# A kernel's opening: phase pieces shared by two selector halves, the first fold ahead of the transposes' copies, eight chunks' rate rows loaded first, 34 exponentials ahead of the transposes

## The chip, the cores and the metric

The kernel runs on one core of a Trainium2 chip. The core has five engines that run side by side, each through its own list of instructions in order: TensorE (PE, matrix products and transposes), VectorE (DVE), ScalarE (ACT), GpSimd (POOL) and SyncE (SP), which here only starts transfers. ACT and POOL start transfers too, and a transfer then runs on the core's DMA engines. Engines meet through semaphores, set by a scheduler that knows which tile each instruction reads and writes.

The metric is the time of one execution in microseconds of device time; less is better. Of the kernel before, three timed runs and one profiled execution are at hand.

## What is computed

The reference is one layer with its gradients. With `xn` the layer norm of `A_u` (2048 tokens, 576 channels):

```python
logdA = dt * (A_re + 1j * A_im)                  # dt = exp(log_dt), 576 x 128
K = einsum("dn,dnl,dn->dl", Cc, exp(logdA * l), dt * Bc).real   # l = 0..2047
s = irfft(rfft(xn) * rfft(K)) + xn * Dskip       # a convolution along the tokens
g = silu(silu(xn @ w1) * (xn @ w3) @ w2)         # 576 -> 4608 -> 576
out = x + s * g
```

Twelve gradients by a given `grad_out` follow, for `A_u`, the eight parameters of the state space part and the three weights. Inputs and outputs are bf16.

## The kernel before

The work has four stages, one behind the other on PE: an opening called `prologue`, the forward of both branches woven together (`ffn_hidden` with `ssm_forward`), the output product with the backward's start, and the backward. Only the opening is touched. It prepares what the forward needs:

- **Magnitudes.** The kernel `K` needs `exp(rate * l)` for 36 chunks of 16 channels. `l` is split into a coarse and a fine part, and a matrix product with a selector (`SELR`, tile `sel_dl`) spreads the rates over both. The rates are cut into three bf16 pieces (`split_rates`), written to the DRAM scratch `PCS_dram`, and read back with another layout into `LR_` (tile `lhs_r`), 48 rows by 36 chunks. `early_exps` then makes 54 blocks: two products (PE, `e_ps`), one exponential (ACT, `E_k`), one store (SP, `E_dram`). Chunks up to `TWICE` = 8 use rows 0 to 47 with a second product, the later ones also rows 64 to 111, which a fourth transfer (`lhs_r<-lhs_r`) copies from the first.
- **Phases.** `param_phases` reduces `A_im * dt / 2 pi` to turns (`thr`). For the two halves of the forward's selector (`SEL`, made by `build_selectors`) it also needs 64 times that, reduced again (`th64`). Both are cut into three pieces by `split3`, on DVE, and written to `PCS_dram` rows 0 and 1 by POOL. The forward reads them as `lhs_t` in `ssm_kernel`.
- **Layer norm.** Even token blocks are loaded straight (`xt<-in_A_u`), odd ones reversed by way of the DRAM scratch `odd_A_u`, on POOL's queue. DVE takes statistics (`ln_stats`, first the even, later the odd ones), roots them, and scales 16 tiles into `xn_bf`. `ln_turn` transposes them (PE into `t_ps`, two buffers; DVE copies `xnT<-t_ps`), ten groups `c` of them, and `ln_fold(b)` makes sums and differences of token blocks (`xt<-xn_bf`, two instructions).
- **Spectra.** `early_spectrum(n)`, n = 0 to 15, makes two groups of eight products from the folded tiles, each group copied out by DVE (from `t_ps`) or ACT (from `e_ps`); here such a group is called a half.

The order is written out by hand. `self.V`, `self.S` and `self.sy` are chains: what is called on them keeps the order of the code on DVE, ACT and SP. `lead` chains the products on PE in the same way. `early_exps` is a generator: `TURN` = 30 of its 54 steps come first, with one surplus product each, then one step behind each transposed group (10) and one behind each half of a spectrum (14, seven spectra). After that come `WT` (two groups of transposes, eight ACT instructions) and the nine spectra that are left; then PE takes up the forward with `pg<-wmB_w,xnT`.

Since PE's order is fixed, a transposed group that waits for a free `t_ps` buffer holds up all exponentials' products behind it.

Of the kernel before, what the change touches and what calls it, by code (L numbers as in the profile page):

```python
# [11 lines left out]
ALU = mybir.AluOpType  # L12
# [86 lines left out]


class K:
    LEAD, SPAN, KG, TURN, TWICE = 1, 38, (4, 6.9), 30, 8
    BACK = ((49, 0), (54, 0), (64, 2), (69, 1))

    def __init__(self, tc, aps: dict, dbg: dict | None = None):
# [208 lines left out]
    def prologue(self, matp, selp, xp, gate):  # L314
# [12 lines left out]
        with pool(name="par_tmp", bufs=1) as tmp, pool(name="par_pc", bufs=2) as pcp, pool(name="sel_tmp", bufs=1) as st, \  # L327
# [32 lines left out]
            rho = tmp.tile([P, DT, N], FP32, name="rho")  # L360
            mul(self.V, rho, self.A_re, dt_b)
            pc = self.split_rates(tmp, rho)
            for k in range(3):
                self.sy.dma_start(out=LR_[k * 16:(k + 1) * 16], in_=self.PCS_dram[2, k].rearrange("(k p) n -> p k n", p=16))
            self.sy.dma_start(out=LR_[64:112, self.TWICE:], in_=LR_[0:48, self.TWICE:])
            pw = eps.tile([P, 1024], FP32, name="e_ps")
            for k in range(16):
# [17 lines left out]
            self.ln_root([*range(LT)], small, last)  # L385
            self.ln_scale(even)
            self.ln_scale(odd)
            self.param_weights(tmp, dt_b, gq)
            self.dma_engines, self._dma_i = [self.sy], 0
            exps = self.early_exps(SELR, LR_, ep, eps)  # L390
# [5 lines left out]
            for k, tiles in enumerate((even, odd)):  # L396
                for c, _ in enumerate(self.ln_turn(tiles, tps)):
                    next(exps)
                    if 5 * k + c == 6:
                        self.ln_fold(0)  # L400
            self.pre(44)
            for n in range(7):
                if n in (2, 5):
                    self.ln_fold(1 + n // 5)
                for _ in spectrum(n, 1, 1):
                    next(exps, None)
            for _ in exps:
# [6 lines left out]
            for src, dsts in ((self.Wr, ((0, 0, 1.0 / 512), (1, 1, -1.0 / 512))), (self.Wi, ((0, 1, -1.0 / 512), (1, 0, -1.0 / 512)))):  # L414
# [3 lines left out]
                for (v, r, sc) in dsts:  # L418
                    for h in range(2):
                        self.S.mul(out=WT[:, v].rearrange("p e r h d u -> p r h e d u")[:, r, h],  # L420
                                   in_=pt[:, h * D // 2:(h + 1) * D // 2].rearrange("p (e d) -> p e d", d=2)[:, :, :, None]
                                   .to_broadcast([P, D // 4, 2, 2]), mul=sc)
            for n in range(7, 16):
                if n == 10:
                    self.ln_fold(3)
                for _ in spectrum(n, int(n < 10), int(n != 10)):
                    pass

    def param_weights(self, tmp, dt_b, q):
# [12 lines left out]
    def param_phases(self, tmp, dt_b):  # L442
        nc, DT, N = self.nc, self.cfg.DT, self.cfg.N
        V = self.V
        thp = tmp.tile([P, DT, N], FP32, name="thp", tag="t1")
        V.scalar_tensor_tensor(out=thp[:], in0=self.A_im[:], scalar=1.0 / (2 * PI), in1=dt_b, op0=ALU.mult, op1=ALU.mult)
        yield
        t = tmp.tile([P, DT, N], FP32, name="sr_t", tag="sr_r1")
        thr = tmp.tile([P, DT, N], FP32, name="thr", tag="rho")
        V.tensor_scalar(out=t[:], in0=thp[:], scalar1=MAGIC, scalar2=-MAGIC, op0=ALU.add, op1=ALU.add)  # L450
        yield
        V.tensor_tensor(out=thr[:], in0=thp[:], in1=t[:], op=ALU.subtract)
        yield
        th64 = tmp.tile([P, DT, N], FP32, name="th64", tag="t1")
        V.tensor_scalar(out=t[:], in0=thr[:], scalar1=64.0, scalar2=MAGIC, op0=ALU.mult, op1=ALU.add)
        yield
        V.tensor_scalar(out=t[:], in0=t[:], scalar1=-MAGIC, scalar2=None, op0=ALU.add)
        yield
        V.scalar_tensor_tensor(out=th64[:], in0=thr[:], scalar=64.0, in1=t[:], op0=ALU.mult, op1=ALU.subtract)
        yield  # L460
        for q, src in enumerate((thr, th64)):
            pc = self.pcp.tile([P, 3, DT, N], BF16, name="pc")
            for _ in self.split3(tmp, src, pc):
                yield
            for dst, part in self.split_rows(q, pc, slice(0, 3)):
                nc.gpsimd.dma_start(out=dst, in_=part)

    def split3(self, tmp, r, pc):
        for k in range(3):
# [107 lines left out]
    def build_selectors(self, st, selp):  # L577
        cfg = self.cfg
        AV, BV, DC = cfg.AV, cfg.BV, 16
        QW, PW = DC * BV, DC * AV  # L580
        val = self.sel_dl
        self.SEL = selp.tile([P, 2, QW // 2 + PW], BF16, name="SEL")
        o = QW + 2 * PW
        self.V.scalar_tensor_tensor(out=val[:, o:], in0=val[:, o:], scalar=self.sel_pm[:, 0:1], in1=self.sel_val[:, o:],
                                    op0=ALU.is_equal, op1=ALU.mult)
        rq = st.tile([P, 1], FP32, name="rq")
        rp = st.tile([P, 1], FP32, name="rp")
        rc = st.tile([P, 1], FP32, name="rc")
        self.V.tensor_scalar(out=rq[:], in0=self.pcol[:], scalar1=48.0, scalar2=None, op0=ALU.is_lt)
        self.V.tensor_scalar(out=rp[:], in0=self.pcol[:], scalar1=64.0, scalar2=None, op0=ALU.is_ge)  # L590
        self.V.tensor_scalar(out=rc[:], in0=self.pcol[:], scalar1=112.0, scalar2=None, op0=ALU.is_lt)
        self.V.tensor_tensor(out=rp[:], in0=rp[:], in1=rc[:], op=ALU.mult)
        self.V.tensor_tensor(out=rp[:], in0=rp[:], in1=rq[:], op=ALU.add)
        rs = st.tile([P, 2], FP32, name="rs")
# [101 lines left out]
    def ssm_kernel(self, T0, TK, ps, ps1):  # L696
        nc, cfg = self.nc, self.cfg
        D, N = cfg.D, cfg.N
        AV, BV = cfg.AV, cfg.BV
        DC = 16  # L700
        NCH = D // DC
        TW = DC * (AV + BV)
        GE = 6
        assert NCH % GE == 0 and AV == 2 * cfg.LT
        with self.pool(name="kg_e", bufs=4) as ep, \
                self.pool(name="kg_l", bufs=2) as lp, \
                self.pool(name="kg_qv", bufs=4) as qvp, \
                self.pool(name="kg_sb", bufs=2) as sb, self.pool(name="kg_dft", bufs=1) as dp, \
                self.pool(name="kg_ks", bufs=2) as self.ksp:
            prev, Es, LT_ = [], [], None  # L710
            self.marks = []
            for ch in range(NCH):
                yield T0 + TK * ch
                self.at(T0 + TK * ch)
                if ch == 10:
                    self.dft_phase_rows(dp)
                if ch in (16, 20, 24, 28):
                    self.dft_kernel_tile(ps, (ch - 16) // 4)
                while len(Es) < min(ch + 3, NCH):
                    c = len(Es)  # L720
                    self.at(T0 + TK * (ch - 0.5) if ch else T0)
                    if c % GE == 0:
                        LT_ = lp.tile([P, GE, N], BF16, name="lhs_t")
                        nc.gpsimd.memset(LT_[:], 1.0)
                        for k in range(3):
                            for q, r0 in enumerate((0, 64)):
                                nc.sync.dma_start(out=LT_[r0 + k * DC:r0 + (k + 1) * DC],
                                                  in_=self.PCS_dram[q, k, c * DC:(c + GE) * DC, :].rearrange(
                                                      "(k p) n -> p k n", p=DC))
                    E = ep.tile([P, TW], BF16, name="E_l")  # L730
                    el = nc.sync.dma_start(out=E[:], in_=self.E_dram[c // 2, :, c % 2 * TW:(c % 2 + 1) * TW])
                    if c == 0:
                        self.kg_load = el
                    if c in (8, 18, 20, 22, 24):
                        self.conv_loads(el, (8, 18, 20, 22, 24).index(c))
                    Es.append((E, LT_))
                self.at(T0 + TK * ch)
                E, lhs = Es[ch]
                qv = self.kgen_chunk(ch, E, lhs[:, ch % GE, :], self.SEL, sb, qvp, ps)
                prev.append(qv)  # L740
                if ch >= 2:
                    self.kgen_sum(ch - 2, prev.pop(0), ps1, T0 + TK * ch, TK)
            for i in range(2):
                yield T0 + TK * (NCH + 0.5 * i)
                self.kgen_sum(NCH - 2 + i, prev.pop(0), ps1, T0 + TK * (NCH + 0.5 * i), TK * 0.5)
# [1514 lines left out]
```

## Time and profile before

| What | us |
|---|---|
| three timed runs: lowest, median, highest | 1645.04, 1669.88, 1679.92 |
| the profiled execution, its own time | 1652.46 |
| its span, first to last instruction | 1650.7 |
| PE busy in it | 1574.6 |
| the opening: start to the first `pg` product | 96.10 |

The rows that the argument rests on are shown where it uses them. A row of the timeline has the start in us, the duration from first to last of a merged group, the engine, the line of the kernel (L86 and L674 are helpers through which the chains issue), what is written and read, and how many instructions (x). In brackets stands the idle time of that engine just before, and what ended it. "PEclk" is the granted clock of TensorE as a share of the full one.

### The profile page before, as it was taken

To read this page: it belongs to the slowest core of one execution; us is meant where nothing else is said; L and a number is where in the kernel's file an instruction comes from. 1 tells how busy PE (TensorE), PEld (TensorE's weight loads), DVE (VectorE), ACT (ScalarE), POOL (GpSimd) and SP (SyncE) were. 2 spreads that over 40 slices of the span, in tenths; PEclk is the share of its full clock that TensorE was granted. 3 is DMA by queue.
4 is the path that set the end of the run, shared out by engine and by line. 5 is a ranking of instruction groups with operands and counts; after the bars stand their busy time and mean duration, and the time that the engine had idled before them with its cause. 6 is when DMAs were issued, how large, how long until landed. Compare 5 with 4: busy or idle time off the path is not lost. (4 is left out here: it accounts for less than half of the span.)

```text
span 1650.7 us, 34338 instructions
## 1 busy us (share of the span) xinstructions
PE 1574.6 (95%) x13327; PEld 1148.8 (70%) x13327; DVE 1390.7 (84%) x2150; ACT 836.4 (51%) x1517; POOL 474.0 (29%) x778
## 2 busy tenths in 40 slices
PE   6899999999999999999999999989999998999997
PEld 2454444444457777788888888878888876888875
DVE  9879999799966656998969999679999945788887
ACT  6789999766642116556565565545555401000101
POOL 7746766532342110111110111111111233123131
PEclk9999999999999999999999999999999999999999
DMA  7899999998999997676695756899998999999991
GB/s 229 313 334 374 378 370 384 380 271 246 325 280 220 240 208 214 173 228 192 186 270 159 217 184 179 197 226 264 246 234 247 234 235 246 233 223 238 231 239 52
DMA packets 621038, 408.57 MB, mean 248 GB/s; under 512 B 424555, under 2 KB 562235, under 8 KB 616267
## 3 DMA queue, kind: packets, MB, share of 16 engines
q1 hardware_dynamic: 565184, 274.01, 66.2%
q0 software_dynamic: 33472, 114.23, 20.7%
q10 hardware_dynamic: 22218, 18.14, 3.8%
q8 instruction: 104, 1.70, 0.4%
q14 instruction: 60, 0.48, 0.1%
HBM read 128.52 MB, written 189.06 MB: 192 GB/s over the span
## 5 line engine op out<-in xcount | busy, mean ns | idle before, releaser
L1961 PEld LDWEIGHTS <-xn_bf 128*128 128x128 bf16 x2304 | 224.3, 98 | 36.4 <-issue 10.2
L2016 PEld LDWEIGHTS <-acts 128*128 128x128 bf16 x1970 | 192.3, 98 | 48.3 <-issue 0.2
L1520 DVE TENSOR_TENSOR pr_q<-et_ps,pz 128x1024 f32<-128x1024 f32 x144 | 175.9, 1222 | 39.1 <-PE et_ps L1515 23.0
L1946 POOL DMA_DIRECT2D out_dram<-gw x72 | 47.2, 656 | 538.0 <-ACT gw L1963 318.6
L1117 PEld LDWEIGHTS <-xnT 128*128 128x128 bf16 x1152 | 107.7, 98 | 127.4 <-issue 20.1
L1523 DVE TENSOR_REDUCE S_all<-pr_q 128x32 f32<-128x1024 f32 x144 | 175.2, 1217 | 3.2
L1895 PE MATMUL ph<-w2T,goT 128*128 128x256 bf16 x1440 | 172.2, 274 | 1.6 <-ACT gh L1898 1.6
L2016 PE MATMUL px<-wT,acts 128*128 128x288 bf16 x1242 | 160.9, 287 | 0.0
L1117 PE MATMUL pg<-wmB_w,xnT 128*128 128x512 bf16 x576 | 155.9, 379 | 1.1 <-DVE g_t L1136 0.6
L1895 PEld LDWEIGHTS <-goT 128*128 128x128 bf16 x1440 | 140.0, 98 | 20.0 <-issue 3.1
L1936 PE MATMUL pgw<-go_o,h_n 128*128 128x288 bf16 x1152 | 152.3, 286 | 1.1 <-ACT gw L1942 1.0
L1117 PE MATMUL pu<-wmB_w,xnT 128*128 128x512 bf16 x576 | 149.7, 379 | 0.0
L1961 PE MATMUL pgw<-gu_n,xn_bf 128*128 128x256 bf16 x1152 | 133.5, 272 | 5.3 <-ACT gw L1942 4.8
L1936 PEld LDWEIGHTS <-h_n 128*128 128x128 bf16 x1152 | 111.9, 98 | 29.2 <-issue 2.1
L1961 PE MATMUL pgw<-gg_n,xn_bf 128*128 128x256 bf16 x1152 | 130.2, 273 | 0.4 <-ACT gw L1963 0.4
L1898 ACT CAST gh<-ph 128x512 bf16<-128x512 f32 x144 | 80.7, 589 | 89.5 <-PE ph L1895 82.2
L1132 ACT ACTIVATE s_t<-pg 128x512 bf16<-128x512 f32 x144 | 88.3, 613 | 54.5 <-PE pu L1126 42.3
L2135 ACT ACTIVATE go<-gx 128x576 bf16<-128x576 f32 x15 | 10.2, 683 | 181.6 <-DVE gx L2085 172.8
L807 POOL COPY KT<-k_s 64x128 bf16<-64x128 bf16 x144 | 85.0, 590 | 52.0 <-ACT k_s L804 47.3
L2016 PE MATMUL px<-wA,acts 128*128 128x288 bf16 x728 | 96.3, 288 | 0.0
L1137 ACT CAST u_t<-pu 128x512 bf16<-128x512 f32 x144 | 87.3, 606 | 6.2 <-PE pu L1117 6.2
L1146 POOL DMA_DIRECT2D G_dram<-g_t x72 | 51.5, 715 | 116.5 <-ACT g_t L1134 91.7
(331 smaller groups left out, 3189.2 us busy)
## 6 DMA issues: line engine op xcount, KB each, us to landing
U_dram<-u_t POOLq DMA_DIRECT2D x72, 256.0 KB, 6.0
H_dram<-h_t SPq DMA_DIRECT2D x72, 256.0 KB
G_dram<-g_t POOLq DMA_DIRECT2D x72, 256.0 KB, 5.8
Q_dram<-q_k SPq DMA_DIRECT2D x36, 512.0 KB
gg_n<-G_dram POOLq DMA_DIRECT2D x18, 1024.0 KB, 6.7
h_n<-U_dram POOLq DMA_DIRECT2D x18, 1024.0 KB, 8.8
GG_dram<-gg_n SPq DMA_DIRECT2D x36, 512.0 KB
GU_dram<-gu_n SPq DMA_DIRECT2D x36, 512.0 KB
```

What stands on the lines that cost most here:

```text
L807: nc.gpsimd.tensor_copy(out=KT[64 * hf:64 * hf + 64, :, ch // 9, h, d1:d1 + 8], in_=ks[64 * h:64 * h + 64, :, h, hf].rearrange("p d a -> p ...
L1117: ins = nc.tensor.matmul(pt[:], lhsT=xnT[:, c, ts], rhs=wm[w][:, c, :], start=(q == 0 and c == 0), stop=(q == 1 and c == nfull - 1))
L1132: nc.scalar.activation(out=s_t[:, :, q, :], in_=pgv, func=ACT.Silu)
L1137: self.gate_last = nc.scalar.copy(out=u_t[:, :, q, :], in_=puv)
L1146: self.u_stores[step] = nc.gpsimd.dma_start(out=dst[fb * ng:(fb + 1) * ng, :, i0:i0 + NT, :].rearrange("g p t f -> p g (t f)"), in_=src[:] ...
L1520: nc.vector.tensor_tensor(out=pr[:].rearrange("p r k e -> p r (k e)"), in0=T[x][:].rearrange("p z k h j a -> p (z k h j a)")[:, None].to_b ...
L1523: nc.vector.tensor_reduce(out=self.S_all[:].rearrange("p r (h c) -> p r h c", h=2)[:, :, :, d0:d0 + 2], in_=pr[:].rearrange("p r k (h j a) ...
L1895: self.pe_last = nc.tensor.matmul(ph[j][:, k, :].rearrange("p (a f) -> p a f", f=P), lhsT=lw, rhs=rh, start=(n == 0), stop=(n == nfull))
L1898: self.sc(lambda: nc.scalar.copy(out=gh[:, j], in_=ph[j][:]))
L1936: self.pe_last = nc.tensor.matmul(pgw[pi_][:, 0:pw], lhsT=hn[:, tt, fl * P:(fl + 1) * P], rhs=go_o[:, tt, po:po + pw], start=(tt == 0), st ...
L1961: self.pe_last = nc.tensor.matmul(pw_[:, 0:FG], lhsT=self.xn_bf[:, tt, c * P:(c + 1) * P], rhs=nat[:, tt, :], start=(tt == 0), stop=(tt == ...
L2016: self.pe_last = nc.tensor.matmul(px[pi_][:, 0:pw], lhsT=acts[i][:, ai, fi, :], rhs=w[:, po:po + pw], start=(n == 0), stop=(n == len(steps ...
```

## The change

```diff
-    LEAD, SPAN, KG, TURN, TWICE = 1, 38, (4, 6.9), 30, 8
+    LEAD, SPAN, KG, TURN, TWICE = 1, 38, (4, 6.9), 34, 8
...
-            for k in range(3):
-                self.sy.dma_start(out=LR_[k * 16:(k + 1) * 16], in_=self.PCS_dram[2, k].rearrange("(k p) n -> p k n", p=16))
+            for c0, c1 in ((0, self.TWICE), (self.TWICE, D // 16)):
+                for k in range(3):
+                    self.sy.dma_start(out=LR_[k * 16:(k + 1) * 16, c0:c1],
+                                      in_=self.PCS_dram[2, k, 16 * c0:16 * c1].rearrange("(k p) n -> p k n", p=16))
...
             self.ln_scale(odd)
+            self.ln_fold(0)
             self.param_weights(tmp, dt_b, gq)
...
                     next(exps)
-                    if 5 * k + c == 6:
-                        self.ln_fold(0)
             self.pre(44)
-            for n in range(7):
-                if n in (2, 5):
-                    self.ln_fold(1 + n // 5)
+            for n in range(5):
+                if n == 2:
+                    self.ln_fold(1)
                 for _ in spectrum(n, 1, 1):
                     next(exps, None)
...
-            for n in range(7, 16):
-                if n == 10:
-                    self.ln_fold(3)
-                for _ in spectrum(n, int(n < 10), int(n != 10)):
+            for n in range(5, 16):
+                if n in (6, 10):
+                    self.ln_fold(n // 4 + 1)
+                for _ in spectrum(n, int(n < 8), int(n != 10)):
                     pass
...
-        th64 = tmp.tile([P, DT, N], FP32, name="th64", tag="t1")
-        V.tensor_scalar(out=t[:], in0=thr[:], scalar1=64.0, scalar2=MAGIC, op0=ALU.mult, op1=ALU.add)
+        pc = self.pcp.tile([P, 3, DT, N], BF16, name="pc")
+        for _ in self.split3(tmp, thr, pc):
+            yield
+        for dst, part in self.split_rows(0, pc, slice(0, 3)):
+            nc.gpsimd.dma_start(out=dst, in_=part)
+        p1 = self.pcp.tile([P, 3, DT, N], BF16, name="pc")
+        t = tmp.tile([P, DT, N], FP32, name="sr_t", tag="sr_r1")
+        V.tensor_scalar(out=t[:], in0=pc[:, 0], scalar1=64.0, scalar2=MAGIC, op0=ALU.mult, op1=ALU.add)
...
-        V.scalar_tensor_tensor(out=th64[:], in0=thr[:], scalar=64.0, in1=t[:], op0=ALU.mult, op1=ALU.subtract)
+        V.scalar_tensor_tensor(out=p1[:, 0], in0=pc[:, 0], scalar=64.0, in1=t[:], op0=ALU.mult, op1=ALU.subtract)
         yield
-        for q, src in enumerate((thr, th64)):
-            pc = self.pcp.tile([P, 3, DT, N], BF16, name="pc")
-            for _ in self.split3(tmp, src, pc):
-                yield
-            for dst, part in self.split_rows(q, pc, slice(0, 3)):
-                nc.gpsimd.dma_start(out=dst, in_=part)
+        for dst, part in self.split_rows(1, p1, slice(0, 1)):
+            nc.gpsimd.dma_start(out=dst, in_=part)
...
+        self.V.tensor_scalar(out=rs[:, 0:1], in0=self.pcol[:], scalar1=80.0, scalar2=63.0, op0=ALU.is_ge, op1=ALU.mult)
+        self.V.tensor_tensor(out=rp[:], in0=rp[:], in1=rs[:, 0:1], op=ALU.add)
...
-                                                  in_=self.PCS_dram[q, k, c * DC:(c + GE) * DC, :].rearrange(
+                                                  in_=self.PCS_dram[q if k == 0 else 0, k, c * DC:(c + GE) * DC, :].rearrange(
```

The factor 64 of the second and third piece goes into the selector (two more instructions of one column in `build_selectors`), so only the first piece is reduced and stored again.

On DVE, in `param_phases`, the order changes as follows (`pc` is the tile of pieces, `sr_r` the rest that is still to be cut; `sr_t` holds whole turns).

```order
-L86 SCALAR_TENSOR_TENSOR th_343<-thr,sr_t 128x640
-L86 CAST pc<-thr 128x640
-L86 TENSOR_TENSOR sr_r_349<-thr,pc 128x640
-L86 CAST pc<-sr_r_349 128x640
-L86 TENSOR_TENSOR sr_r_352<-sr_r_349,pc 128x640
-L86 CAST pc<-sr_r_352 128x640
-L86 CAST pc<-th_343 128x640
-L86 TENSOR_TENSOR sr_r_363<-th_343,pc 128x640
-L86 CAST pc<-sr_r_363 128x640
-L86 TENSOR_TENSOR sr_r_366<-sr_r_363,pc 128x640
-L86 CAST pc<-sr_r_366 128x640
+L86 SCALAR_TENSOR_TENSOR pc<-pc,sr_t 128x640
```

The five instructions that cut `th` are gone, the cut of `thr` (removed here) now stands ahead of the reduction, and what is reduced goes straight into a piece; the odd tiles' statistics follow directly in both.

On DVE again, between the scaling and the spectra, first before, then after (`xt_152` is token block 0, `xt_153` block 1 and so on).

```order
L86 TENSOR_SCALAR xn_bf<-xt_155,rstd,negmr 128x576 x2
L86 MEMSET Wr 128x1
L86 MEMSET Wi 128x1
L86 COPY xnT<-t_ps 128x8x128 x4
L86 CAST xnT<-t_ps 128x8x128
L86 COPY xnT<-t_ps 128x8x128 x2
L86 TENSOR_TENSOR xt_152<-xn_bf 128x1152 x2
L86 COPY xnT<-t_ps 128x8x128 x2
L86 CAST xnT<-t_ps 128x8x128
L86 CAST u_e<-t_ps 128x2x288 x4
L86 TENSOR_TENSOR xt_153<-xn_bf 128x1152 x2
L86 CAST u_e<-t_ps 128x2x288 x6
```

```order
L86 TENSOR_SCALAR xn_bf<-xt_155,rstd,negmr 128x576 x2
L86 TENSOR_TENSOR xt_152<-xn_bf 128x1152 x2
L86 MEMSET Wr 128x1
L86 MEMSET Wi 128x1
L86 COPY xnT<-t_ps 128x8x128 x4
L86 CAST xnT<-t_ps 128x8x128
L86 COPY xnT<-t_ps 128x8x128 x4
L86 CAST xnT<-t_ps 128x8x128
L86 CAST u_e<-t_ps 128x2x288 x4
L86 TENSOR_TENSOR xt_153<-xn_bf 128x1152 x2
L86 CAST u_e<-t_ps 128x2x288 x8
L86 TENSOR_TENSOR xt_154<-xn_bf 128x1152 x2
```

The fold of block 0 moved from between the seventh and the eighth copy to ahead of the first, and the fold of block 2 (`xt_154`) now follows eight casts instead of six.

On SP the rates come in two groups of three loads; before there were three, and the copy into rows 64 to 111 stood right behind them. This is the order now.

```order
L86 DMA lhs_r<-PCS_dram 16x8x128 x3
L86 DMA lhs_r<-PCS_dram 16x28x128 x3
L674 DMA E_dram<-E_k 128x1024 x3
L86 DMA lhs_r<-lhs_r 48x3584
L674 DMA E_dram<-E_k 128x1024 x32
```

The copy `lhs_r<-lhs_r` is now issued behind the stores of the first three exponentials. On PE and ACT nothing in the forward or behind it changes its order.

More of the change, by code (lines that the diff above doesn't have):

```diff
@@ L588, in build_selectors @@
         rc = st.tile([P, 1], FP32, name="rc")
+        rs = st.tile([P, 2], FP32, name="rs")
         self.V.tensor_scalar(out=rq[:], in0=self.pcol[:], scalar1=48.0, scalar2=None, op0=ALU.is_lt)
@@ L591, in build_selectors @@
         self.V.tensor_scalar(out=rc[:], in0=self.pcol[:], scalar1=112.0, scalar2=None, op0=ALU.is_lt)
+        self.V.tensor_scalar(out=rs[:, 0:1], in0=self.pcol[:], scalar1=80.0, scalar2=63.0, op0=ALU.is_ge, op1=ALU.mult)
+        self.V.tensor_tensor(out=rp[:], in0=rp[:], in1=rs[:, 0:1], op=ALU.add)
         self.V.tensor_tensor(out=rp[:], in0=rp[:], in1=rc[:], op=ALU.mult)
         self.V.tensor_tensor(out=rp[:], in0=rp[:], in1=rq[:], op=ALU.add)
-        rs = st.tile([P, 2], FP32, name="rs")
         self.V.tensor_scalar(out=rs[:, 0:1], in0=self.pcol[:], scalar1=112.0, scalar2=192.0, op0=ALU.is_equal,
```

## The prediction

> **What bounds the kernel, and what bounds its opening.** I read the page first, then the busy time by stretches.
>
> ```profile
> span 1650.7 us, 34338 instructions
> PE 1574.6 (95%) x13327; PEld 1148.8 (70%) x13327; DVE 1390.7 (84%) x2150; ACT 836.4 (51%) x1517; POOL 474.0 (29%) x778
> ...
> 100.00:350.00 250.00, 247.35 (x1714) 111.11 (x1713) 230.93 (x374) 225.07 (x453) 153.94 (x243) 1.00 1.02 365
> ```
>
> A row of the stretches gives, after the limits, the length, then PE, weight loads, DVE, ACT and POOL busy, then the granted clock, the share of the DMA engines and GB/s. Behind the opening PE is busy nearly all the time (247.35 of 250 us in this stretch, 95% of the span with the opening in it), in an order that the change leaves alone. So the change is worth what it moves the first forward product on PE, and that shift passes to the end.
>
> Next I read ACT's timeline in the opening, since 54 exponentials are its longest work.
>
> ```profile
> 16.59 1.28 ACT L86 ACT_TABLE_LOAD   x1
> 19.81 1.02 ACT L86 ACTIVATE E_k<-e_ps 128x1024 bf16<-128x1024 f32 x1 [1.95 <-PE e_ps L674]
> 21.95 1.02 ACT L86 ACTIVATE E_k<-e_ps 128x1024 bf16<-128x1024 f32 x1 [1.11 <-PE e_ps L674]
> ...
> 46.61 7.71 ACT L86 ACTIVATE E_k<-e_ps 128x1024 bf16<-128x1024 f32 x8 [0.37 <-ACT E_k L86]
> 56.14 6.67 ACT L86 ACTIVATE E_k<-e_ps 128x1024 bf16<-128x1024 f32 x7 [1.81 <-issue]
> 66.64 1.02 ACT L86 ACTIVATE E_k<-e_ps 128x1024 bf16<-128x1024 f32 x1 [3.83 <-issue]
> 68.45 1.02 ACT L86 ACTIVATE E_k<-e_ps 128x1024 bf16<-128x1024 f32 x1 [0.79 <-PE e_ps L674]
> 70.26 4.95 ACT L86 ACTIVATE E_k<-e_ps 128x1024 bf16<-128x1024 f32 x5 [0.79 <-PE e_ps L674]
> 75.83 5.68 ACT L86 ACTIVATE E_k<-e_ps 128x1024 bf16<-128x1024 f32 x6 [0.62 <-PE e_ps L674]
> 82.58 1.94 ACT L86 ACTIVATE E_k<-e_ps 128x1024 bf16<-128x1024 f32 x2 [1.06 <-DMA E_dram<-E_k]
> ```
>
> One exponential takes 7.71/8 = 0.964 us in a row of them. The 54 start at 19.81 and end at 84.52. The two large holes, 1.81 and 3.83 us, are to be explained by PE and DVE.
>
> ```profile
> 9.91 6.54 PE L368 MATMUL e_ps<-pc 128*128 128x512 bf16 x16 [6.60 <-DVE pc L86]
> 18.78 1.43 PE L674 MATMUL e_ps<-sel_dl,lhs_r 128*128 128x512 bf16 x4 [2.32 <-DMA lhs_r<-PCS_dram]
> ...
> 52.54 0.59 PE L674 MATMUL e_ps<-sel_dl,lhs_r 128*128 128x512 bf16 x2
> 55.01 0.61 PE L674 MATMUL t_ps<-ident_bf,xn_bf 128*128 128x128 bf16 x8 [1.88 <-DVE xnT L86]
> 64.52 1.06 PE L674 MATMUL t_ps<-ident_bf,xn_bf 128*64 128x128 bf16 x16 [2.90 <-DVE xnT L86]
> 95.60 0.66 PE L674 MATMUL t_ps<-xt,cCS 128*128 128x144 bf16 x8
> 96.10 1.03 PE L1117 MATMUL pg<-wmB_w,xnT 128*128 128x512 bf16 x4
> ...
> 33.16 0.76 DVE L86 CAST pc<-th 128x640 bf16<-128x640 f32 x1
> 36.81 0.80 DVE L86 BATCH_NORM_STATS2 stats<-xt 128x6 f32<-128x288 bf16 x2
> 54.28 0.68 DVE L86 COPY xnT<-t_ps 128x1024 bf16<-128x1024 bf16 x1
> 60.07 3.79 DVE L86 TENSOR_TENSOR xt<-xn_bf 128x1152 bf16<-128x1152 bf16 x2
> 63.79 1.27 DVE L86 COPY xnT<-t_ps 128x1024 bf16<-128x1024 bf16 x2
> 72.52 1.42 DVE L86 TENSOR_TENSOR xt<-xn_bf 128x1152 bf16<-128x1152 bf16 x2
> 86.19 4.49 DVE L86 CAST u_e<-t_ps 128x576 bf16<-128x576 f32 x6 [2.84 <-PE t_ps L674]
> ```
>
> Both holes are PE's waits for a DVE copy. The first copy starts at 54.28, when the scaling is done, and PE's third transposed group 0.73 us later. The second wait is the fold at 60.07, 3.79 us between two copies. A third wait, 2.32 us, stands at the start, for the rates.
>
> **The parts of the change.**
>
> *Eight chunks first.* PE's surplus products end at 16.45 (9.91 + 6.54) and ACT is free at 17.87 (16.59 + 1.28). Eight of 36 chunks are 2/9 of the bytes, so I estimate the rates there by 16.5: the first exponential comes at 17.9 instead of 19.81. The second then also loses its wait of 1.11. The bounds are 0 (the load's time is all latency) and 1.95 + 1.11 = 3.1; I take 3.0. Three more loads on SP, and the copy `lhs_r<-lhs_r` behind three stores, come before the 13th exponential, the first to read it, with some 8 us to spare. By itself this part is worth nothing: what ends last next is DVE.
>
> *The phase pieces.* From 33.16 to 36.81 DVE cuts `th`; these 3.65 us go, and the two instructions of one column that are added are much less. But behind them stand the odd tiles' statistics, and POOL tells when these tiles land:
>
> ```profile
> 30.77 2.83 POOL L86 DMA_DIRECT2D xt<-odd_A_u  x4
> ...
> DMA to landing us min/median/max: 5.9/6.5/7.0
> ```
>
> The first is issued at 30.77 and lands 5.9 us later at the earliest, at 36.7; DVE's statistics began at 36.81, with no wait only because DVE came no sooner. So DVE comes 3.6 us earlier and waits 3.6 us. The gain is between 0 and 3.6, I take 0: nothing in the change makes these transfers start earlier. Exponentials that start 3 us earlier also send their stores earlier, against the same transfers. I add 0.6 us for that (0 to 1.4, the middle; 1.4 is the time of two stores' 512 KB at the 365 GB/s of the row 100 to 350).
>
> *The fold ahead of the copies.* It takes 1.42 (row 72.52) to 3.79 (row 60.07). The 3.79 stood beside POOL's products of the weights:
>
> ```profile
> 55.32 2.15 POOL L855 IOTA ph_f<- 1x256 bf16 x1
> 58.49 1.40 POOL L86 TENSOR_TENSOR Wr<-C_re_bf,B_re_bf 128x640 f32<-128x640 bf16 x1
> ```
>
> At 55 to 57 POOL still writes constants of one row, so I take 1.42. The first copy then starts at 54.28 + 0.6 + 1.42 = 56.3, and the third transposed group at 57.0. The second hole goes altogether.
>
> *34 exponentials.* Four more come ahead of the transposes, 4 x 0.964 = 3.86 us of ACT, and their four surplus products hide in PE's waits for ACT. PE's last product ahead of the wait ended at 52.54 + 0.59 = 53.13; now at 53.13 + 3.86 - 3.0 = 54.0. PE then waits from 54.0 to 57.0, which is 3.0 us.
>
> What such a wait costs beyond itself is told by the granted clock, by single microseconds:
>
> ```profile
> 54.00:55.00 1.00, 0.00 (x0) 0.00 (x0) 1.00 (x5) 0.32 (x1) 0.87 (x4) 1.00 0.98 377
> ...
> 64.00:65.00 1.00, 0.48 (x10) 0.48 (x11) 1.00 (x2) 0.00 (x0) 1.00 (x2) 0.50 1.09 358
> 70.00:71.00 1.00, 1.00 (x11) 0.88 (x10) 0.15 (x2) 0.74 (x1) 1.00 (x2) 0.77 0.66 254
> ```
>
> Behind the wait of 1.88 the clock stayed full; behind that of 2.90 it was at half by 64 and until about 70.5, and ACT's exponentials came every 1.81 us (66.64, 68.45, 70.26). A wait of 3.0 us is past the second, so I take the half clock, with the same cost: from the copy at 63.79 to the exponential at 66.64 are 2.85 us, then two steps of 1.81. The Trainium skill's page "TensorE: Matmul & The Clock Gate", section "What's actually happening", lets the clock fall after an idle window of about 3.4 us that runs free of the kernel. The trace does not bear that out as it stands, since 2.90 us were enough. By that rule the clock would stay full here, which is the first rival below.
>
> *Spectra.* Four halves move behind the exponentials. PE takes 0.50 us for one there (95.60 to 96.10), so 2.0 us. The fold of block 2 now stands among six casts that DVE did without a break (4.49 us, row 86.19): 1.42 at most, 0 if other work covers it; DVE sets the pace there, so I take 1.4.
>
> **The sum.** Exponential 37 starts at 56.3 + 2.85 = 59.15, the 39th at 62.8. Then 16 x 0.964 = 15.4 and the two small holes of before, 0.62 and 1.06: they end at 79.9, against 84.52. From their end to the first `pg` there were 11.58 us; now 11.58 + 2.0 + 1.4 = 15.0. The forward starts at 94.9 instead of 96.10, so 1.2 us are gained. Against the profiled execution's own 1652.46 that is 1651.3. That execution lies 17 us below the median of the timed runs (1669.88), and those spread over 35 us for reasons that this profile does not show. I refer the forecast to the middle of the four times, (1652.46 + 1669.88) / 2 = 1661.2, and get 1660.0.
>
> **Rivals.**
>
> - *The clock stays full.* The wait is a little shorter or falls differently than the one that ended at 64.52. Then exponential 37 comes 1.86 us behind the copy (54.28 to 56.14), at 58.2, and 18 x 0.964 + 1.7 later, at 77.2, they end; forward at 92.2, a gain of 3.9: 1657.3. For it speaks that the wait of 1.88 us cost no clock; against it that my 3.0 is longer than both. The page named above would have it so.
> - *The odd tiles are early too.* Less DMA work ahead of them lets DVE keep its 3.6 us. Then ACT sets the pace: exponential 37 at 46.61 + 7.71 + 3.86 - 3.0 = 55.2, end at 74.2, forward at 89.2, a gain of 6.9: 1654.3. Against it: the loads are issued at 30.77 behind the reversal in DRAM, which the change leaves alone.
> - *Slower: the fold is long.* If the fold takes 3.79 where it now stands, because DVE and POOL are in each other's way there too, the first copy starts at 58.7, exponential 37 at 61.5, they end at 82.2, and the forward starts at 97.2: 1.1 us later, 1662.3. It decides once the first copy starts later than 57.5. For it speaks POOL's own instruction of 2.15 us at 55.32, long for one row.
> - *No effect.* The forward's first chunks wait for something that does not move with the opening, and 0 is left: 1661.2. Against it: their loads are issued behind the last exponential's store, which comes earlier.
>
> **How the numbers follow.** Chances: my forecast 0.42, full clock 0.30, odd tiles early 0.08, slower by the fold 0.14, no effect 0.06. All of them lie within 7 us of the time before, 0.4%, while about 2% (33 us) is what a measurement of this kernel can tell from no change. So same has 0.96, and faster and slower 0.02 each, which is the spread of the runs alone. The range takes the lowest and the highest run with the outermost cases, 1645.04 - 6.9 = 1638 and 1679.92 + 1.1 = 1681, and leaves out the last 2 us above, as that run with that case is unlikely: 1638 to 1679.
>
> **What would show it.** In the profile after: the first `E_k` at about 17.9; DVE idle for about 3.6 us ahead of the odd tiles' statistics, ended by a transfer; the fold right behind the scaling, at 1.42; a wait of about 3 us of PE ahead of the third transposed group, and the granted clock at 0.50 behind it; no fold between the copies; the last exponential's end near 80; the first `pg` near 95 (96.10 before). I am wrong in the main step if the statistics start near 33 us, and in the term of the clock if it stays at 1.00.

## The result, and the profile after

| | before | after |
|---|---|---|
| median of 22 timed runs each, us | 1668.63 (1645.04 to 1688.18) | 1646.85 (1638.38 to 1667.46) |
| ratio after / before | | 0.9933, 95% interval 0.9904 to 0.9962 |
| the profiled execution's own time, us | 1652.46 | 1646.07 |
| first `pg` product in it, us | 96.10 | 91.82 |

The changed kernel was 0.7% faster in this comparison, which is less than the 2% that count as a difference here. The ratio compares only the runs within 1.5% of the fastest of their kernel, so it is not the quotient of the two medians (0.987). The profiled executions differ by 6.39 us, and 96.10 - 91.82 = 4.28 us of that are gained in the opening. The span and PE's line of the page of the changed kernel, then one row of its stretches:

```profile
span 1644.3 us, 34303 instructions
PE 1569.0 (95%) x13280; PEld 1147.0 (70%) x13331; DVE 1384.0 (84%) x2145; ACT 837.3 (51%) x1519; POOL 470.7 (29%) x778
```

```profile
100.00:350.00 250.00, 244.59 (x1680) 110.89 (x1708) 230.40 (x373) 223.14 (x449) 152.99 (x243) 1.00 1.03 362
```

PE still bounds what lies behind the opening (244.59 of 250 us; 247.35 before). ACT's timeline of the opening:

```profile
17.88 1.94 ACT L86 ACTIVATE E_k<-e_ps 128x1024 bf16<-128x1024 f32 x2
...
28.95 2.10 ACT L86 ACTIVATE E_k<-e_ps 128x1024 bf16<-128x1024 f32 x2 [0.32 <-PE e_ps L679]
32.39 6.03 ACT L86 ACTIVATE E_k<-e_ps 128x1024 bf16<-128x1024 f32 x6 [1.34 <-PE e_ps L679]
39.52 1.02 ACT L86 ACTIVATE E_k<-e_ps 128x1024 bf16<-128x1024 f32 x1 [1.10 <-DMA E_dram<-E_k]
40.77 4.96 ACT L86 ACTIVATE E_k<-e_ps 128x1024 bf16<-128x1024 f32 x5 [0.23 <-DMA E_dram<-E_k]
45.97 20.12 ACT L86 ACTIVATE E_k<-e_ps 128x1024 bf16<-128x1024 f32 x21 [0.24 <-ACT E_k L86]
...
72.92 3.77 ACT L86 ACTIVATE E_k<-e_ps 128x1024 bf16<-128x1024 f32 x4 [1.32 <-DMA UH_dram<-u_e]
```

Two things are to be seen. The exponentials start 1.93 us earlier (17.88 against 19.81), and the 11th 3.23 us earlier: it starts at 28.95, and in the profile of before the row that begins with it starts at 32.18:

```profile
32.18 14.06 ACT L86 ACTIVATE E_k<-e_ps 128x1024 bf16<-128x1024 f32 x14 [0.32 <-PE e_ps L674]
```

But before the 13th (32.39) they lose 1.34 us and before the 19th 1.10. Counted through the rows, the 25th starts at 45.97, and at 46.61 before: 0.64 us of the lead are left. And both large holes of before are gone: 21 exponentials follow one another from 45.97 on, and the last ends at 72.92 + 3.77 = 76.69 (84.52 before). SP's queue, PE and DVE tell why, in the same timeline:

```profile
21.58 0.61 SPq L86 DMA_DIRECT2D lhs_r<-lhs_r  x1
...
31.49 1.46 PE L679 MATMUL e_ps<-sel_dl,lhs_r 128*128 128x512 bf16 x6 [1.77 <-DMA lhs_r<-lhs_r]
54.52 0.61 PE L679 MATMUL t_ps<-ident_bf,xn_bf 128*128 128x128 bf16 x8
56.27 0.61 PE L679 MATMUL t_ps<-ident_bf,xn_bf 128*128 128x128 bf16 x8
91.82 1.03 PE L1122 MATMUL pg<-wmB_w,xnT 128*128 128x512 bf16 x3
...
36.56 0.82 DVE L86 BATCH_NORM_STATS2 stats<-xt 128x6 f32<-128x288 bf16 x2 [2.55 <-DMA xt<-odd_A_u]
54.07 1.41 DVE L86 TENSOR_TENSOR xt<-xn_bf 128x1152 bf16<-128x1152 bf16 x2
55.41 0.68 DVE L86 COPY xnT<-t_ps 128x1024 bf16<-128x1024 bf16 x1
```

The hole ahead of the 13th exponential is PE's wait for the copy `lhs_r<-lhs_r`, issued at 21.58. The third transposed group starts at 56.27 with no wait at all: the first copy is done at 55.41 + 0.68 = 56.09, and PE came no sooner. The clock stayed full there, as one row of the stretches shows:

```profile
56.00:57.00 1.00, 0.95 (x12) 0.71 (x11) 0.81 (x3) 1.00 (x2) 0.91 (x2) 1.00 0.76 295
```

### The profile page after: what moved, and what is told of

It reads as the page before. It is cut to its first block, busy times and chain, and to the rows that moved or that the text cites. A ratio compares the mean times of both kernels' runs of the same rounds, so it can differ in the third digit from the quotient of the medians.

```text
span 1644.3 us, 34303 instructions
## 1 busy us (share of the span) xinstructions
PE 1569.0 (95%) x13280; PEld 1147.0 (70%) x13331; DVE 1384.0 (84%) x2145; ACT 837.3 (51%) x1519; POOL 470.7 (29%) x778
## 5 line engine op out<-in xcount | busy, mean ns | idle before, releaser
L1122 PE MATMUL pg<-wmB_w,xnT 128*128 128x512 bf16 x539 | 150.2, 379 | 3.6 <-DVE g_t L1141 0.9
L1137 ACT ACTIVATE s_t<-pg 128x512 bf16<-128x512 f32 x144 | 88.5, 614 | 55.4 <-PE pu L1131 43.2
```

Of the source, the lines that this page charges most:

```text
L1122: ins = nc.tensor.matmul(pt[:], lhsT=xnT[:, c, ts], rhs=wm[w][:, c, :], start=(q == 0 and c == 0), stop=(q == 1 and c == nfull - 1))
L1137: nc.scalar.activation(out=s_t[:, :, q, :], in_=pgv, func=ACT.Silu)
```

## Experiments

Twelve runs were made, two of them of a kernel without an edit. The time of the opening (first `pg`) is read from one profile each. The kernel before had 96.10 there, and 95.23 in the second profile that one of the runs below gave; the changed kernel had 91.82, and 92.24 in its second. So a difference under about 0.9 us between two kernels tells nothing.

### Each part alone

**The fold moved, on the kernel before.**

```diff
             self.ln_scale(odd)
+            self.ln_fold(0)
...
-                    if 5 * k + c == 6:
-                        self.ln_fold(0)
```

> Of the change only the fold of block 0 ahead of the copies. Theory A (the fold between the copies made the second hole, and that is where the gain is): the first copy starts near 55.7 us (54.28 + 1.4), PE waits some 3.3 us ahead of the third transposed group, the second hole is gone; the first pg product starts near 92.1 with the clock full, near 94.6 with it at half behind that wait (96.10 in before, 91.82 in after). Theory B (the gain comes from the shorter chain on DVE ahead of the odd tiles): it needs the phase pieces, so the first pg stays near 96.

First `pg` at 97.13, time 1664.5 (before on that chip: 1669.31). PE and DVE in its timeline:

```profile
57.02 0.61 PE L673 MATMUL t_ps<-ident_bf,xn_bf 128*128 128x128 bf16 x8 [3.85 <-DVE xnT L86]
...
54.94 1.41 DVE L86 TENSOR_TENSOR xt<-xn_bf 128x1152 bf16<-128x1152 bf16 x2
```

and the granted clock around that wait, the third column from the end:

```profile
56.00:57.00 1.00, 0.00 (x0) 0.00 (x0) 1.00 (x5) 0.00 (x0) 1.00 (x1) 1.00 0.73 279
57.00:58.00 1.00, 0.97 (x12) 0.74 (x12) 0.90 (x2) 0.00 (x0) 1.00 (x1) 0.97 0.07 27
58.00:59.00 1.00, 1.00 (x10) 0.86 (x9) 0.41 (x2) 0.85 (x1) 0.91 (x2) 0.50 0.01 4
```

The fold takes 1.41 us in its new place, but it is in the way of the first copy. PE's wait of 1.88 grows to 3.85, and the clock falls. The 94.6 expected for this case was missed by 2.5 us: the first copy comes at 56.29 in place of 55.7, and later the exponentials wait 1.82 us at 71.10 and 2.50 at 75.54 for transfers, where the kernel before has 0.62 and 1.06. Why these waits are longer is open. Alone, this part gains nothing in the opening.

**34 exponentials, on the kernel before.**

```diff
-    LEAD, SPAN, KG, TURN, TWICE = 1, 38, (4, 6.9), 30, 8
+    LEAD, SPAN, KG, TURN, TWICE = 1, 38, (4, 6.9), 34, 8
...
-            for n in range(7):
+            for n in range(5):
```

> Of the change only 34 exponentials and the spectra that move with them. Theory A: the first wait of PE goes, the fold between the copies still costs its hole of 3 to 4 us, and four halves and a fold move behind the exponentials: the first pg starts between 96 and 98. Rival C (34 exponentials are what keeps PE busy and the clock full, and so the gain): no half clock, the first pg near 92.

First `pg` at 93.06, the earliest of the four parts: the 96 to 98 expected was wrong, and the rival's 92 is nearer. The single execution took 1687.46 us as a whole all the same; PE waited long behind the opening: 9.6 us for `hcA<-H_dram`, 10.1 for `gz<-gK_dram`, 13.6 for `gw` (1.0, 8.5 and 4.8 in the first profile of before). Its opening, in the timeline of ACT, PE and DVE:

```profile
67.26 6.62 ACT L86 ACTIVATE E_k<-e_ps 128x1024 bf16<-128x1024 f32 x7 [2.07 <-issue]
...
66.00 0.64 PE L674 MATMUL t_ps<-ident_bf,xn_bf 128*64 128x128 bf16 x16 [2.00 <-DVE xnT L86]
...
62.45 2.89 DVE L86 TENSOR_TENSOR xt<-xn_bf 128x1152 bf16<-128x1152 bf16 x2
```

The first hole is gone, because PE comes to the transposes later than DVE. The fold, 2.89 us beside POOL's products, still makes the second one, without a fall of the clock.

**The rates in two steps, on the kernel before.**

```diff
+            for c0, c1 in ((0, self.TWICE), (self.TWICE, D // 16)):
+                for k in range(3):
+                    self.sy.dma_start(out=LR_[k * 16:(k + 1) * 16, c0:c1],
...
```

> Of the change only the two groups of rate loads. Theory A: the first exponential at 17.9 us instead of 19.81, the copy lhs_r<-lhs_r lands near 31.5 and PE waits 1.5 to 2 us for it, so that the lead is lost by the 13th exponential; the first pg stays at 95.5 to 96.5. Rival: the lead of 2 to 3 us lasts to the end, the first pg near 93.5.

First `pg` at 95.16, time 1653.74. The first exponential starts at 17.88, the 25th at 46.35 (46.61 before): the lead of 1.9 us is 0.3 by then.

**The phase pieces, on the kernel before.**

```diff
-        for q, src in enumerate((thr, th64)):
...
+        for dst, part in self.split_rows(1, p1, slice(0, 1)):
+            nc.gpsimd.dma_start(out=dst, in_=part)
```

> Of the change only the phase pieces. Theory A: DVE waits 2.5 us or more for the odd tiles, the first copy starts at 54.0 to 54.3, the first pg at 95.5 to 96.3. Theory B: the first copy starts near 51 and the first pg 2 to 3 us earlier than in before, near 93.5.

First `pg` at 95.08, time 1665.4. DVE's timeline, the odd tiles' statistics:

```profile
36.20 0.82 DVE L86 BATCH_NORM_STATS2 stats<-xt 128x6 f32<-128x288 bf16 x2 [1.81 <-DMA xt<-odd_A_u]
```

DVE comes earlier and waits, 1.81 us where 2.5 or more were expected. The first copy starts at 54.18, and at 54.28 before. This part and the last lie within 0.2 us of the second profile of the kernel before (95.23).

### How much is chance, and where the lead goes

**The kernel before against itself,** with no edit.

> The kernel before, unchanged, against itself: what the timing calls a difference where there is none. Theory D (what the whole kernel gains beyond the 4.3 us of the opening is chance, since the late stages wait for transfers by a different amount in every execution): the ratio lies within 0.995 to 1.005, single times spread over 30 us or more, and this second profile shows PE's waits for transfers behind 500 us (acts<-GG_dram, gz<-gK_dram, hcA<-H_dram) at another sum than the 11.2 us of the first two in the first profile. Rival E (the change shortens the late stages too): the waits behind 500 us are the same in both profiles of before, within 2 us.

Median 1659.58 against 1654.6 of the same kernel beside it, ratio 1.0042 (1.0006 to 1.0079). PE's waits from 110 us on (in total, times, longest), from the first profile of the kernel before:

```profile
PE et_ps L1515 <- DMA gz<-gK_dram: 8.5, 2, 4.4
PE pgw L1961 <- ACT gw L1942: 4.8, 13, 1.7
```

and from the second:

```profile
PE pgw L1961 <- ACT gw L1942: 18.5, 13, 13.8
...
PE et_ps L1515 <- DMA gz<-gK_dram: 3.5, 2, 3.2
```

One kernel, two executions: 13.7 us more for `gw`, 5.0 less for `gz`. The waits of the late stages alone move the time by more than the whole opening's gain, and an interval that leaves out 1 for equal kernels is narrower than the real uncertainty.

**The changed kernel with the loads as before,** the two loops over the chunks undone:

```diff
-            for c0, c1 in ((0, self.TWICE), (self.TWICE, D // 16)):
...
+            for k in range(3):
+                self.sy.dma_start(out=LR_[k * 16:(k + 1) * 16], in_=self.PCS_dram[2, k].rearrange("(k p) n -> p k n", p=16))
```

> The changed kernel with the rates loaded in one piece again. Theory A: the lead of the first exponentials is lost in the changed kernel by the 13th, so nothing is lost here: first exponential 19.8 us, no wait for the copy lhs_r<-lhs_r, PE reaches the transposes within 1 us of the changed kernel (54.52), the first pg at 91.5 to 92.8 (91.82 in the changed kernel). Rival: the early loads are worth their 2 us, the first pg near 94. Whole time against before: ratio 0.990 to 0.998 by either.

First `pg` at 92.34; median 1653.57, ratio to before 0.9992 (0.995 to 1.0033). The first exponential starts at 20.08, the 25th at 46.57, 0.6 us behind the changed kernel, although it began 2.2 us later.

**The copy `lhs_r<-lhs_r` issued ahead of the first store,** in the changed kernel, by an order between the two:

```diff
-            self.sy.dma_start(out=LR_[64:112, self.TWICE:], in_=LR_[0:48, self.TWICE:])
+            self.rates_in = self.sy.dma_start(out=LR_[64:112, self.TWICE:], in_=LR_[0:48, self.TWICE:])
...
+            with self.tc.issue_after(self.rates_in.ins):
+                self.e_stores.append(...)
```

> The changed kernel with the copy lhs_r<-lhs_r issued ahead of the exponentials' stores instead of behind three of them. Theory A: PE no longer waits 1.77 us for it; PE reaches the transposes 1 to 2 us sooner (near 53) and then waits 1 to 2 us for DVE, since the odd tiles set the time of the copies; the first pg stays at 91 to 92 with the clock full, near 93.5 if the wait costs the clock. Rival: the exponentials set the time, the first pg near 90.

First `pg` at 92.82; median 1650.04, ratio 0.9986 (0.9944 to 1.0028). PE no longer waits for the copy. ACT's timeline:

```profile
28.63 1.02 ACT L86 ACTIVATE E_k<-e_ps 128x1024 bf16<-128x1024 f32 x1 [1.06 <-DMA E_dram<-E_k]
30.45 1.02 ACT L86 ACTIVATE E_k<-e_ps 128x1024 bf16<-128x1024 f32 x1 [0.80 <-DMA E_dram<-E_k]
...
46.74 10.73 ACT L86 ACTIVATE E_k<-e_ps 128x1024 bf16<-128x1024 f32 x11 [0.22 <-ACT E_k L86]
```

The same time is now lost to the stores: an exponential waits until an older block has left its buffer. The row from 46.74 on begins with the 25th. So it isn't the copy's place that takes the lead. PE doesn't come sooner to the transposes, and neither the 91 to 92 expected nor the rival's 90 came about.

**The odd tiles' reversal first on POOL's queue as well,** on top of the last edit:

```diff
+        q.dma_start(out=self.odd["A_u"][:], in_=self.turned(self.aps["A_u"].flatten_outer_dims()))
         tiles = [self.dmat(pool, n, setter=self.V) for n in names]
...
-            if n == "B_re":
-                q.dma_start(out=self.odd["A_u"][:], in_=self.turned(self.aps["A_u"].flatten_outer_dims()))
```

> As copy_early, and the reversal of the odd token blocks in DRAM issued first on POOL's queue, ahead of the five parameter loads. If the odd tiles' landing is what hides the phase pieces' gain on DVE (theory A), the odd statistics start at 33 to 35 us instead of 36.56, the first copy at 52 to 54 instead of 55.41, and with the exponentials' lead the first pg comes at 88.5 to 90.5. Rival (the odd tiles are held by the stores' traffic, not by the place in the queue): the statistics stay near 36.5 and the first pg near 91.8.

First `pg` at 97.14; median 1648.43, ratio 0.998 (0.9943 to 1.0017). The profiled execution is the longest of its runs (1691.55 us; they begin at 1641.71), so the order of its events counts here, not their size. Its timeline:

```profile
33.96 0.81 DVE L86 BATCH_NORM_STATS2 stats<-xt 128x6 f32<-128x288 bf16 x2
...
31.59 1.02 ACT L86 ACTIVATE E_k<-e_ps 128x1024 bf16<-128x1024 f32 x1 [4.02 <-DMA E_dram<-E_k]
35.80 1.94 ACT L86 ACTIVATE E_k<-e_ps 128x1024 bf16<-128x1024 f32 x2 [3.18 <-DMA E_dram<-E_k]
```

The statistics start 2.6 us earlier and without a wait, and the exponentials wait 7.2 us for their stores. In this execution what one stream of transfers gained, the other paid, and neither the 88.5 to 90.5 expected nor the rival's 91.8 came about. Since it is one execution, and the longest, that price isn't shown for the others.

### The changed kernel with one part undone

**The changed kernel once more,** with no edit.

> The changed kernel once more, beside the kernel before. If the whole gain of the first comparison (ratio 0.9933) is the change's own, the ratio is 0.991 to 0.996 again. Theory D (only the 4.3 us of the opening are the change's, 0.26% of the time; the rest of the first difference came from late waits that vary between executions) expects 0.997, and anything from 0.993 to 1.001, since the kernel before against itself gave 1.0042. The first pg stands at 91.5 to 92.7 in the profile by both; a first pg past 94 would say that the opening's gain is chance too.

Median 1645.69 against 1655.75, ratio 0.9959 (0.9924 to 0.9993); first `pg` at 92.24. This ratio lies in the ranges of both theories and doesn't decide between them; the opening's gain came again.

**The phase pieces undone** (as in the kernel before, with the other three parts):

```diff
+        for q, src in enumerate((thr, th64)):
...
-        for dst, part in self.split_rows(1, p1, slice(0, 1)):
-            nc.gpsimd.dma_start(out=dst, in_=part)
```

> The changed kernel with the phase pieces as before (both halves of the selector have their own, three more casts and their differences on DVE). If the pieces are hidden behind the landing of the odd tiles, as forecast, those tiles' statistics start at 36.5 to 37.6 with a wait under 0.5 us (2.55 in the changed kernel), the first copy at 55.4 to 56.5, and the first pg at 91.8 to 92.9. The rival, that the pieces give DVE what the diff removes (3.65 us), has the statistics at 40, and the first pg past 94.5.

First `pg` at 92.39, time 1640.8 (one run). DVE's timeline:

```profile
36.70 0.82 DVE L86 BATCH_NORM_STATS2 stats<-xt 128x6 f32<-128x288 bf16 x2
```

The statistics start within 0.14 us of the changed kernel's 36.56, now without its wait of 2.55. The pieces were covered by the odd tiles' landing.

**30 exponentials again:**

```diff
-    LEAD, SPAN, KG, TURN, TWICE = 1, 38, (4, 6.9), 34, 8
+    LEAD, SPAN, KG, TURN, TWICE = 1, 38, (4, 6.9), 30, 8
...
-            for n in range(5):
+            for n in range(7):
```

> The changed kernel with 30 exponentials ahead of the transposes and the halves of the spectra as before. PE is done with its products some 3.9 us earlier, near 52, and waits 3.5 to 4 us for the first copy (55.4). If such a wait takes the clock down, as in the prediction's main case, a window there shows 0.5 to 0.8, exponentials come every 1.8 us behind it, and the first pg stands at 94 to 97. If only the wait itself counts (the clock full), the first pg stands at 91.5 to 92.5, and the four exponentials are worth nothing beside the early fold.

First `pg` at 96.20, time 1650.92 (one run). PE and ACT in its timeline:

```profile
56.27 1.01 PE L679 MATMUL t_ps<-ident_bf,xn_bf 128*128 128x128 bf16 x8 [3.65 <-DVE xnT L86]
...
58.22 1.02 ACT L86 ACTIVATE E_k<-e_ps 128x1024 bf16<-128x1024 f32 x1 [4.42 <-issue]
59.92 1.02 ACT L86 ACTIVATE E_k<-e_ps 128x1024 bf16<-128x1024 f32 x1 [0.68 <-PE t_ps L679]
61.88 7.61 ACT L86 ACTIVATE E_k<-e_ps 128x1024 bf16<-128x1024 f32 x8 [0.94 <-PE e_ps L679]
```

and its clock:

```profile
54.00:55.00 1.00, 0.00 (x0) 0.00 (x0) 1.00 (x3) 0.00 (x0) 0.91 (x3) 0.99 0.78 297
55.00:56.00 1.00, 0.00 (x0) 0.00 (x0) 1.00 (x4) 0.00 (x0) 1.00 (x1) 0.50 0.37 139
...
61.00:62.00 1.00, 1.00 (x8) 0.56 (x7) 1.00 (x1) 0.12 (x1) 1.00 (x1) 0.60 0.20 76
62.00:63.00 1.00, 1.00 (x16) 0.76 (x14) 0.76 (x2) 1.00 (x2) 0.92 (x2) 1.00 0.49 186
```

The third transposed group starts at 56.27, as in the changed kernel, but PE has waited 3.65 us for it, the clock is at half from 55 to nearly 62, and three exponentials come 1.7 and 2.0 us apart. With the other three parts in place and these four exponentials missing, nothing of the gain is left (96.20 against 96.10 and 95.23).

**The fold back between the copies:**

```diff
-            self.ln_fold(0)
...
+                    if 5 * k + c == 6:
+                        self.ln_fold(0)
```

> The changed kernel with the fold of block 0 back between the copies. The first copy starts 1.4 us earlier, near 54.0, and PE waits for no copy there; the fold then takes 2.8 to 3.8 us beside POOL's products and makes one hole of about 2 us in the exponentials, as in the kernel with the 34 exponentials alone. If that hole is the fold's price the first pg stands at 92.8 to 94; if ACT or the spectra have slack for it, it stays at 91.5 to 92.3.

First `pg` at 92.41, time 1638.34 (one run). PE and DVE in its timeline:

```profile
64.98 0.64 PE L680 MATMUL t_ps<-ident_bf,xn_bf 128*64 128x128 bf16 x16 [1.67 <-DVE xnT L86]
...
61.76 2.56 DVE L86 TENSOR_TENSOR xt<-xn_bf 128x1152 bf16<-128x1152 bf16 x2
```

The fold takes 2.56 us there and makes one hole in ACT's row (1.74 us at 66.24), but the first `pg` comes only 0.2 to 0.6 us later than in the two profiles of the changed kernel. That is below the 92.8 to 94 expected for a hole that costs its length, and less than can be told from nothing. The hole takes the place of later waits: the changed kernel's exponentials wait 0.45, 0.22 and 1.32 us behind that point, these only 0.57, and they end at 77.31 against 76.69.

## Why the forecast was right in its range and wrong in its main step

The time, 1646.85, lies in the range of 1638 to 1679, and that no difference of 2% would show was right. The forecast itself was 1660.0, and its likeliest case didn't come about: the second one did, "the clock stays full", with `pg` forecast at 92.2 and measured at 91.82. That the number fits so well is in part luck: this case kept a wait of PE and only left the clock full, while in the changed kernel there is no wait at all, because the lead was lost.

**The step that failed: "the copy `lhs_r<-lhs_r` … with some 8 us to spare", and with it the lead of 3.0 us that the sum carried to the transposes.** The lead was there at first (3.23 us at the 11th exponential). But the copy was issued at 21.58, and PE had it at 31.49, 9.9 us later and 1.77 us later than PE needed it. The exponentials' own stores took most of what was left (1.10 us before the 19th). The table gives the start of the 1st and the 25th exponential in the profiles:

| kernel | 1st | 25th |
|---|---|---|
| before, two profiles | 19.81, 20.20 | 46.61, 47.08 |
| loads alone | 17.88 | 46.35 |
| changed, two profiles | 17.88, 17.88 | 45.97, 46.01 |
| changed, loads as before | 20.08 | 46.57 |
| changed, copy ahead of the stores | 17.88 | 46.74 |

Whenever the row starts in these kernels, its 25th comes at 46 to 47 (the one profile with the odd tiles first has it later still, at 51.32). The DMA engines were full in that stretch before the change (the second column from the end), in the profile of before:

```profile
32.00:47.00 15.00, 12.16 (x47) 4.34 (x46) 14.41 (x44) 14.07 (x15) 13.10 (x26) 1.00 1.03 356
```

and after:

```profile
32.00:47.00 15.00, 10.42 (x40) 3.76 (x40) 11.84 (x41) 12.87 (x14) 12.17 (x27) 1.00 1.02 368
```

While the copy was under way in the changed kernel, from 21.58 to 31.49, their share was 0.98. Before the change ACT, at 14.07 of 15 us, was close behind the DMA engines; started earlier, it only waited more (12.87 busy). With 0.64 us of lead in place of 3.0 the working gives PE's end at 53.13 + 3.86 - 0.64 = 56.35, and the profile shows 55.84 + 0.38 = 56.22. That is later than the first copy's end (56.09), so there was no wait, and no half clock. Whether more buffers for the stores would keep some of the lead was not tried.

**The clock's term was right as a mechanism.** The run with 30 exponentials had the wait that the forecast feared, 3.65 us, and the half clock, which began within the wait. First `pg` 96.20 against 91.82 and 92.24 prices the four exponentials, the wait, the clock and the later waits of the row (1.83 us at 71.33 and 1.23 at 74.50) together at 4.0 to 4.4 us. How much of it is the clock's isn't shown. The Trainium skill's page "TensorE: Matmul & The Clock Gate", section "What's actually happening", has the clock fall after an idle window of about 3.4 us. By that rule a wait of 3.0 us leaves it full; the runs do not bear that out, as waits of 2.03 and 2.44 us brought it down (last section).

**Where the gain comes from.** The forecast gave the rates and the phase pieces nothing, and did not part the fold's share from the exponentials'. The runs put the gain on the four exponentials more ahead of the transposes: alone they give 93.06, the other three parts without them 96.20. Taking out any one of the other three leaves 92.34 to 92.41, within 0.6 us of the changed kernel.

**The phase pieces at nothing: right.** DVE waited 2.55 us instead of working (forecast 3.6: of the 3.65 us of cutting, 2.80 went, since DVE was done at 34.01 in place of 36.81); both runs on this part agree. The 0.6 us added for a later landing (the middle of 0 to 1.4 would be 0.7) did not show: DVE's statistics on the odd tiles started 0.25 us earlier (36.56 against 36.81).

**The eight chunks' rates: the first exponential right** (17.9 forecast, 17.88 measured), the second's wait gone, as forecast, and that this part is worth nothing by itself was right as well: 95.16 alone, 92.34 without it.

**The fold: its duration right** (1.42 forecast, 1.41 measured), and the first copy came at 55.41 instead of 56.3: 0.6 us of that are the later landing that did not come, and 0.2 the scaling's earlier end (54.07 against 54.28). The slower rival by a fold of 3.79 us falls. But the move alone made PE's wait longer and the opening 1.0 to 1.9 us later, which the sum had not told apart from the exponentials that cover it.

**The tail: right.** From the last exponential's end to the first `pg` 91.82 - 76.69 = 15.1 us (15.0 forecast).

**The odd tiles early:** they came early in one run, by another order of the transfers, and in that execution the stores paid for it. Its first `pg` at 97.14 is far from the case's 89.2, but whether the case can be had in a shorter execution isn't shown.

**The whole time.** The opening gives 3.0 to 4.3 us, by the two profiles of each kernel (95.23 - 92.24 and 96.10 - 91.82, rounded), 0.2 to 0.3% of the time. The two comparisons gave 0.7% and 0.4%. The forecast's reference, 1661.2, is one value out of medians of 1668.63, 1654.6 and 1655.75 for the same kernel. Less 4.3 us it would have given 1656.9, still 10 us above the measured time; the three medians lie 14 us apart, so the choice of the reference alone can hold that. From the first `pg` to the end of the span the two profiles of the kernel before take 1554.6 and 1564.2 us, those of the changed kernel 1552.5 and 1545.8: two executions of one kernel differ by 7 to 10 us there, more than the whole gain of the opening, and late waits as those shown are part of that. That the change has a part in them was neither shown nor excluded.

## What to carry to other kernels

Before carrying a head start through a sum, look at the share of the DMA engines in the stretch that it must cross: here they were full, and an engine that started earlier only waited at its output buffers. Parts of one change are not additive when one of them takes away the cover that another needs: the fold ahead of the copies cost 1 to 2 us alone and nothing behind four more exponentials. Time an unchanged kernel against itself before reading a difference of half a per cent.

## What the runs showed of the hardware

- **The clock falls after waits of 2.0 to 2.5 us, though not after all of them.** In the run with the phase pieces alone PE waited 2.03 us up to 54.91, and the granted clock was 0.57 from 56 to 57 and 0.50 from 57 to 59. In the second profile of the kernel before it was 1.00 from 64 to 65 behind a wait of 2.44 us, then 0.75 and 0.50. But waits of 2.00 us (the 34 exponentials alone) and 2.09 us (the loads alone) left it at 1.00. The fall can come about 1 us after PE is back at work (57.02 in the run with the fold alone, half clock from 58), or within the wait (at 55 with 30 exponentials). By rows of 1 us the fall lasted about 3.4 us in some of the cases and twice that in others, whatever the wait was (3.4 behind a wait of 3.85, 6.8 behind one of 2.90). The Trainium skill's page "TensorE: Matmul & The Clock Gate", section "What's actually happening", has windows of about that length that run free of the kernel. The falls fit that, except that a window which is idle only in part must have been enough, since waits of 2.03 to 2.90 us are shorter than a window. How large a part it takes isn't shown.
- **A copy of 336 KB from SBUF to SBUF took 9.9 us** (issued at 21.58, PE's wait for it over at 31.49) in a stretch where the DMA engines were busy with other transfers: their share was 0.98 from 21.58 to 31.49, at 353 GB/s, a pace at which 336 KB are 1.0 us.
- **The fold of the same size took 1.41 us ahead of the copies, and 2.56, 2.89, 3.11 and 3.79 between them** (3.11 and 3.79 in the two profiles of the kernel before). The one of 2.56 us, from 61.76 on, stands beside two of POOL's products (1.65 us from 62.06 on and 1.91 from 63.67 on); the one of 1.41, at 54.07 in the changed kernel, beside instructions of POOL that write constants of one row. POOL's instruction of 2.15 us there did not lengthen it. The Trainium skill's page "SBUF — State Buffer", section "SBUF: two separate sides", lets a DVE instruction with two SBUF inputs and a POOL instruction that reads SBUF shut each other out for a whole instruction; the two places agree with that.
